# Two products of a gated linear attention in 64x64 matmul tiles instead of 64x128

## The chip, the cores and the metric

The kernel runs on one core of a Trainium2 chip. TensorE (PE) multiplies matrices into PSUM; a matmul instruction is preceded by a load of its stationary operand (LDWEIGHTS, shown as PEld). VectorE (DVE), ScalarE (ACT) and GpSimd (POOL) do the elementwise work, and SyncE (SP) issues most of the DMAs. The metric is the device time of one launch in microseconds (us); a comparison of the two kernels resolves about 2%.

## The reference

Per batch and head a 48x48 state is decayed row by row and updated with an outer product at each of 768 steps; the output of a step is the query times the state. The result, 3072 tokens by 384, goes through a gated feed-forward layer.

```python
B, H, S, D = 4, 8, 768, 48
f = 1 / (1 + exp(-f_logit))
for t in range(S):
    state = f[:, :, t, :, None] * state + einsum('bhd,bhe->bhde', k[:, :, t], v[:, :, t])
    y[:, :, t] = einsum('bhd,bhde->bhe', q[:, :, t], state)
x = y.transpose(0, 2, 1, 3).reshape(B * S, H * D)        # 3072 x 384
h = x @ w_in                                             # 384 -> 2048
out = (h * sigmoid(h)) @ w_out                           # 2048 -> 384
```

## The kernel before, in words

The 768 steps are cut into 3 windows of 256 steps, and each window into two chunks of 128. With 4 batches that makes 12 blocks, D = 0 to 11 (window D // 4, batch D % 4). In a block a partition holds a pair of neighbouring steps, r = 0 and 1; partitions 0 to 63 are the first chunk and 64 to 127 the second (f = 0 and 1 in the matmuls). The decays become factors on q and k, so that inside a chunk the attention is a masked product of q and k times v, and only the state is carried from chunk to chunk.

The order of all work is written out by hand in a long string, PLAN, whose tokens are emitted one after the other; a token such as `Y.8.0` is a step kind, a block and a half of the heads (g = 0 or 1, four heads each). Each engine takes its instructions in that order. Buffers come from small pools by class, also decided by the order of the tokens. The steps that matter here:

- SC (line 350): scores q times k, in tiles of 48 rows by 64 columns of the array, 128 moving columns; the two heads of a pair stand on two row halves, the two chunks on two column halves. 16 matmuls per token, 24 tokens.
- AT (line 356, DVE): the mask times the scores, out of PSUM.
- Y (line 364): the second attention product, masked scores times v. The contraction is over the 64 partitions of a chunk f, so two matmuls use the upper and the lower half of the array; each writes 128 partitions (both r of the 64 output pairs) by the 48 columns of one head. 16 matmuls per token, 24 tokens.
- YS (line 371): q times the carried state, added onto Y's PSUM banks, in tiles of 128 rows by 64 columns, 96 moving columns. 8 matmuls per token, 20 tokens.
- YC (line 278): copies the sum out of PSUM.
- DP (line 389): the state product, k times v over a chunk. Two heads x of a pair n are stationary together (128 columns of the array) and both heads' values move (96 columns), so the result is a 128x96 block for each pair whose two off-diagonal quarters belong to no head. 16 matmuls per token for blocks 0 to 7; in the last window only the first chunk is needed, and blocks 8 to 11 have 8 (the function `chunks_with_state`).
- SD (line 394, DVE): adds DP's PSUM bank to the carried state. SU (line 396, POOL or DVE): multiplies by the decay `al`, which is zero in the off-diagonal quarters, and writes the new state in bf16.
- MI and MO (lines 405 and 418): the two feed-forward products, full 128x128 tiles with 256 and 384 moving columns; SI (line 413, ACT) the gate between them.
- W (line 443): products of zeros, in the first part of the kernel alone.

`nc.tensor.matmul` issues one LDWEIGHTS and one MATMUL each time. Where the operands start on partition 64, or where the output does, decides which part of the array is used.

## Time and profile before

| | us |
|---|---|
| median of 3 runs | 176.93 (176.51 to 178.69) |
| profiled execution, whole | 176.33 |
| its span from first to last instruction | 174.61 |
| PE busy | 168.4 |
| ACT / DVE / POOL busy | 123.4 / 101.7 / 72.1 |

The span is what the profile's views divide up; the profiled execution took 1.7 us more than its span. PE's busy time overlaps itself, because a matmul starts streaming while the one ahead is still draining; how fast matmuls follow each other is therefore read from the chain of work that ended last, whose rows give a group of instructions the time until the next group begins. The names in the rows: `ps` is a PSUM bank, `atm` the masked scores, `vb` the values v, `qk` the factored q and k before transposition, `qkT` after it, `st` the state, `sd` state plus product, `yb` the copied output, `hT` the hidden layer.

### The profile page before, as it was taken

Reading aid. Unit: us, or ns where it says so; the run is one execution under the profiler, and the core shown is the slowest. Engines: PE = TensorE matmul, PEld = TensorE weight load, DVE = VectorE, ACT = ScalarE, POOL = GpSimd, SP = SyncE. Lnnn points to the kernel's source line nnn. Section 1 sums busy time; section 2 is a strip of 40 time slices with the busy share of each in tenths; the row PEclk is TensorE's granted clock in tenths of the full one; section 3 lists DMA queues with packets and bytes.
Section 4 is the critical chain, followed back from the end, with each engine's and each line's share of the span. In section 5 each row is a group of like instructions: output and inputs, shape, how many; then the busy total and the mean of one; then the engine's idle time right before and its main releaser. Section 6 shows DMA issues by size and latency. Waiting matters only on the chain.

```text
span 174.6 us, 5617 instructions
## 1 busy us (share of the span) xinstructions
PE 168.4 (96%) x2289; PEld 128.6 (74%) x2289; DVE 101.7 (58%) x248; ACT 123.4 (71%) x287; POOL 72.1 (41%) x121
## 2 busy tenths in 40 slices
PE   7799999999999999999999999999999999999992
PEld 5677788867856788867688767688667788867671
DVE  6389989666447989488494597893678400000010
ACT  5989999898948989696987948769621227763420
POOL 6486752519891784213229260193019220000220
PEclk9999999999999999999999999999999999999999
DMA  5999999999949959999798999899994683000064
GB/s 136 278 283 303 329 350 357 351 277 357 299 93 222 302 137 266 127 272 300 131 282 156 267 271 263 185 223 238 302 108 88 159 168 90 4 0 0 0 144 132
DMA packets 81066, 36.02 MB, mean 206 GB/s; under 512 B 74000, under 2 KB 80272, under 8 KB 81040
## 3 DMA queue, kind: packets, MB, share of 16 engines
q1 hardware_dynamic: 79440, 31.86, 74.6%
q0 software_dynamic: 1024, 3.15, 6.9%
q10 hardware_dynamic: 576, 0.66, 1.1%
q8 instruction: 18, 0.29, 0.7%
q14 instruction: 8, 0.07, 0.1%
HBM read 25.17 MB, written 4.72 MB: 171 GB/s over the span
## 4 chain that ended last, share of the span: by engine, by line
PE 83%; SPq 9%; DMA 4%; DVE 1%; issue 1%; ACT 0%; ACTq 0%
PE ps L418 36%; PE ps L405 33%; SPq L282 7%; DMA wide<-in_k_dram 4%; PE ps L350 3%; PE ps L364 3%; PE ps L371 2%; SPq L434 2%; PE ps L389 2%; PE ps L337 1%; PE ps L298 1%; DVE qk L328 1%; PE ps L379 0%; PE ps L302 0%; DVE wide L317 0%
## 5 line engine op out<-in xcount | busy, mean ns | idle before, releaser
L418 PE MATMUL ps<-w_out_sb,hT 128*128 128x384 bf16 (+2 forms) x400 | 68.1, 320 | 0.0
L405 PE MATMUL ps<-xT,w_in_sb 128*128 128x256 bf16 x576 | 67.1, 273 | 0.0
L405 PEld LDWEIGHTS <-w_in_sb 128*128 128x128 bf16 x576 | 55.4, 98 | 8.6 <-POOL w_in_sb L278 0.2
L413 ACT ACTIVATE hT<-ps 128x512 bf16<-128x512 f32 x88 | 45.8, 626 | 14.7 <-PE ps L405 14.3
L418 PEld LDWEIGHTS <-hT 128*128 128x128 bf16 x400 | 36.9, 98 | 20.7
L356 DVE TENSOR_TENSOR atm<-ps,mask 128x512 bf16<-128x512 f32 x48 | 29.9, 683 | 13.0 <-PE ps L350 12.8
L278 DVE COPY o<-ps 128x384 f32<-128x384 f32 (+1 forms) x11 | 5.9, 541 | 32.2 <-PE ps L418 32.2
L426 POOL DMA_DIRECT2D out_dram<-o x16 | 9.9, 619 | 29.7 <-ACT o L278 26.3
L278 ACT COPY o<-ps 128x384 f32<-128x384 f32 (+1 forms) x14 | 6.4, 465 | 16.2 <-PE ps L418 16.2
L396 POOL TENSOR_TENSOR st<-sd,al 128x384 bf16<-128x384 f32 x13 | 10.9, 845 | 11.9 <-DVE sd L394 11.9
L284 ACT ACTIVATE e<-wide 128x384 f32<-128x384 f32 x24 | 12.2, 520 | 4.7 <-DMA wide<-in_f_logit_dram 3.8
L328 POOL TENSOR_TENSOR qk<-wide,ia 128x192 bf16<-128x192 f32 x22 | 13.2, 621 | 5.4 <-DVE wide L317 4.7
L328 DVE TENSOR_TENSOR qk<-wide,ps 128x192 bf16<-128x192 f32 x48 | 14.1, 347 | 1.7 <-ACT ps L311 0.8
L290 POOL TENSOR_TENSOR s<-lf 128x192 bf16<-128x192 bf16 x15 | 8.5, 578 | 14.3 <-ACT lf L286 14.2
L317 POOL TENSOR_TENSOR wide<-wide,f 128x192 f32<-128x192 f32 x14 | 9.0, 639 | 13.2 <-DMA wide<-in_k_dram 12.2
L328 DVE TENSOR_TENSOR qk<-wide,ia 128x192 bf16<-128x192 f32 x26 | 12.5, 527 | 1.8 <-POOL wide L317 1.7
L319 DVE SCALAR_TENSOR_TENSOR wide<-e,wide 128x192 f32<-128x192 f32 x24 | 10.1, 434 | 4.8 <-DMA wide<-in_q_dram 4.8
L286 ACT ACTIVATE lf<-e 128x384 bf16<-128x384 f32 x24 | 12.2, 525 | 0.3
L447 ACT ACT_TABLE_LOAD x9 | 11.5, 1283 | 0.2
L443 PE MATMUL ps<-idle 128*128 128x256 bf16 x65 | 10.3, 318 | 1.3 <-DVE idle L455 1.3
L278 POOL CAST vb<-wide 128x768 bf16<-128x768 f32 x7 | 6.0, 873 | 12.5 <-DMA wide<-in_v_dram 12.5
L394 DVE TENSOR_TENSOR sd<-ps,st 128x384 f32<-128x384 f32 x16 | 8.3, 551 | 4.0 <-ACT hT L413 2.7
(60 smaller groups left out, 176.1 us busy)
## 6 DMA issues: line engine op xcount, KB each, us to landing
wide<-in_f_logit_dram SPq DMA_DIRECT2D x10, 384.0 KB, 5.0
wide<-in_q_dram SPq DMA_DIRECT2D x10, 384.0 KB, 6.1
wide<-in_k_dram SPq DMA_DIRECT2D x10, 384.0 KB, 5.5
wide<-in_v_dram SPq DMA_DIRECT2D x10, 384.0 KB, 5.5
wide<-in_moe_w_in_dram SPq DMA_DIRECT2D x8, 384.0 KB, 6.1
wide<-in_moe_w_out_dram SPq DMA_DIRECT2D x8, 384.0 KB, 5.9
out_dram<-o POOLq DMA_DIRECT2D x16, 192.0 KB, 3.9
wide<-in_f_logit_dram SPq DMA_DIRECT2D x4, 192.0 KB, 3.3
```

The source lines that it names most:

```text
L278: copy = lambda o, i: E.copy(o, i) if eng == "a" else E.tensor_copy(o, i)
L282: E.dma_start(out=T[0][:, hs], in_=SRC[kind[2]][w, b][:, hs])
L284: nc.scalar.activation(T[1][:, hs], T[0][:, hs], AF.Exp, scale=-1.0)
L286: nc.scalar.activation(T[1][:, hs], T[0][:, hs], AF.Ln, bias=1.0)
L328: E.tensor_mul(T[2][:, g, int(kind == "KI"), :, r, :, 0:d], T[0][:, hs, r * d:r * d + d].rearrange("p (n x) d -> p n x d", x=2), decay.rea ...
L356: nc.vector.tensor_mul(T[2][:, g, x], T[x].rearrange("p (s n c) -> p s n c", s=2, n=2), mask.rearrange("p s r c -> p s (r c)")[:, :, None, ...
L396: E.tensor_mul(T[2].rearrange("p n (x d) -> p n x d", d=d), T[0][:, 0:HD].rearrange("p (n x d) -> p n x d", n=4, d=d) if "ps" in mine[0] e ...
L405: nc.tensor.matmul(h[:, i, 128 * fs.start:128 * fs.stop], w_in_sb[:, j, kk, i * 128:i * 128 + 128], T[0][:, fs, kk], start=(kk == 0), stop ...
L413: nc.scalar.activation(T[1][:, 2 * j:2 * j + 2], T[0].rearrange("p (n c) -> p n c", n=2), AF.Silu)
L418: nc.tensor.matmul(T[1][:, 0:cols.stop - cols.start], T[0][:, n, f * 128:f * 128 + 128], w_out_sb[:, n, cols], start=(n == 0), stop=(n == ...
L443: nc.tensor.matmul(T[0][:, 0:256], idle[:, 0:128], idle[:, 0:256], start=True, stop=True, skip_group_check=True)
L447: nc.scalar.preload_act_table_set(turn[name])
```

## The change

Y and DP are issued in 64x64 tiles. In Y each matmul becomes two, one for each half r of its 128 output partitions; the moving operand (48 columns of v) is the same for both. In DP each matmul becomes two, one for each head x of the pair, and each moves only that head's 48 columns, so the off-diagonal quarters are no longer computed: a state bank holds, on 64 partitions per head, 4 x 48 columns instead of 4 x 96. SD (and SU for the first chunk) read those columns with a stride of zero, so that the 128x384 tile they write has a copy in both places of a pair; the one that belongs to the wrong head is multiplied by the zero in `al`, as before.

```diff
+        heads = lambda x: x.rearrange("p n (x d) -> p n x d", d=d)
+        both_heads = lambda x: x[:, 0:4 * d].rearrange("p (n d) -> p n d", d=d)[:, :, None, :].to_broadcast([128, 4, 2, d])
...
                         for f in range(2):
-                            nc.tensor.matmul(T[2 + f][:, h * d:h * d + d], T[0][64 * f:64 * f + 64, g, x, s, n],
-                                             T[1][64 * f:64 * f + 64, h, s * d:s * d + d],
-                                             start=(h == 0 and s == 0), stop=True, skip_group_check=True)
+                            for r in range(2):
+                                nc.tensor.matmul(T[2 + f][64 * r:64 * r + 64, h * d:h * d + d],
+                                                 T[0][64 * f:64 * f + 64, g, x, s, n, 64 * r:64 * r + 64],
+                                                 T[1][64 * f:64 * f + 64, h, s * d:s * d + d],
+                                                 start=(h == 0 and s == 0), stop=True, skip_group_check=True)
...
                     for f in fs:
-                        nc.tensor.matmul(T[2 + f][:, 2 * d * n:2 * d * n + 2 * d],
-                                         T[0][64 * f:64 * f + 64, n // 2, 1, n % 2, r].rearrange("p x c -> p (x c)"),
-                                         T[1][64 * f:64 * f + 64, 2 * n:2 * n + 2, r * d:r * d + d],
-                                         start=(n == 0 and r == 0), stop=True, skip_group_check=True)
+                        for x in range(2):
+                            nc.tensor.matmul(T[2 + f][64 * x:64 * x + 64, d * n:d * n + d],
+                                             T[0][64 * f:64 * f + 64, n // 2, 1, n % 2, r, x],
+                                             T[1][64 * f:64 * f + 64, 2 * n + x, r * d:r * d + d],
+                                             start=(n == 0 and r == 0), stop=True, skip_group_check=True)
         elif kind == "SD":
-            nc.vector.tensor_add(T[1], T[0][:, 0:HD].rearrange("p (n c) -> p n c", n=4), T[2])
+            nc.vector.tensor_add(heads(T[1]), both_heads(T[0]), heads(T[2]))
         elif kind == "SU":
-            E.tensor_mul(T[2].rearrange("p n (x d) -> p n x d", d=d),
-                         T[0][:, 0:HD].rearrange("p (n x d) -> p n x d", n=4, d=d) if "ps" in mine[0] else T[0].rearrange("p n (x d) -> p n x d", d=d),
+            E.tensor_mul(heads(T[2]), both_heads(T[0]) if "ps" in mine[0] else heads(T[0]),
                          T[1][:, :, a[1]][:, :, :, None].to_broadcast([128, 4, 2, d]))
```

On PE the place where the state products of block 6 end and the scores of block 6 begin (`DP.6 SC.6.0` in PLAN) stands before the change as follows; the two numbers behind a name are partitions by columns of the output, and `ps_130` and `ps_133` are the banks of the two chunks.

```order
L389 LDWEIGHTS qk_99
L389 MATMUL ps_133<-vb_104,qk_99 128x96
L389 LDWEIGHTS qk_99
L389 MATMUL ps_130<-vb_104,qk_99 128x96
L389 LDWEIGHTS qk_99
L389 MATMUL ps_133<-vb_104,qk_99 128x96
L350 LDWEIGHTS qkT_107 [waits DMAHW0_49]
L350 MATMUL ps_131<-qkT_107 64x128 [waits Activation_49]
```

And the same place in the changed kernel, where the lines are numbered 2 to 5 higher:

```order
L394 LDWEIGHTS qk_99
L394 MATMUL ps_130<-vb_104,qk_99 64x48
L394 LDWEIGHTS qk_99
L394 MATMUL ps_130<-vb_104,qk_99 64x48
L394 LDWEIGHTS qk_99
L394 MATMUL ps_133<-vb_104,qk_99 64x48
L394 LDWEIGHTS qk_99
L394 MATMUL ps_133<-vb_104,qk_99 64x48
L352 LDWEIGHTS qkT_107 [waits DMAHW0_49]
L352 MATMUL ps_131<-qkT_107 64x128 [waits Activation_49]
```

Each pair of instructions has become two pairs on the same bank with half the output partitions and half the columns; the waits, the banks and what follows are the same.

On PE the place where the second attention products of block 8 begin behind a feed-forward product (`MO.6.0.2 ... Y.8.0` in PLAN), before the change; `ps_133` and `ps_127` are the banks of the two chunks:

```order
L418 LDWEIGHTS hT_118
L418 MATMUL ps_132<-w_out_sb,hT_118 128x384
L364 LDWEIGHTS atm_108
L364 MATMUL ps_133<-vb_102,atm_108 128x48 [waits DVE_49]
L364 LDWEIGHTS atm_108
L364 MATMUL ps_127<-vb_102,atm_108 128x48 [waits DVE_49]
```

And in the changed kernel, at the same place:

```order
L422 LDWEIGHTS hT_118
L422 MATMUL ps_132<-w_out_sb,hT_118 128x384
L367 LDWEIGHTS atm_108
L367 MATMUL ps_133<-vb_102,atm_108 64x48 [waits DVE_49]
L367 LDWEIGHTS atm_108
L367 MATMUL ps_133<-vb_102,atm_108 64x48
L367 LDWEIGHTS atm_108
L367 MATMUL ps_127<-vb_102,atm_108 64x48 [waits DVE_49]
L367 LDWEIGHTS atm_108
L367 MATMUL ps_127<-vb_102,atm_108 64x48
```

The two matmuls of a round, one for each chunk, have become four, two for each chunk, with the same columns and the waits at the same bank's first matmul.

Over the whole program PE has 5668 rows instead of 4580: 384 more matmuls from Y, 160 more from DP, each with its load. The rows of DVE, ACT, POOL and SP are the same in both kernels, in order, shapes and waits, and PE's waits stand at the same matmuls.

## The prediction

> **What bounds the kernel now.** I read the page's head first, then the shares of the chain of work that ended last, then that chain in order of time.

> ```profile
> span 174.6 us, 5617 instructions
> PE 168.4 (96%) x2289; PEld 128.6 (74%) x2289; DVE 101.7 (58%) x248; ACT 123.4 (71%) x287; POOL 72.1 (41%) x121
> PE 83%; SPq 9%; DMA 4%; DVE 1%; issue 1%; ACT 0%; ACTq 0%
> PE ps L418 36%; PE ps L405 33%; SPq L282 7%; DMA wide<-in_k_dram 4%; PE ps L350 3%; PE ps L364 3%; PE ps L371 2%; SPq L434 2%; PE ps L389 2%; PE ps L337 1%; PE ps L298 1%; DVE qk L328 1%; PE ps L379 0%; PE ps L302 0%; DVE wide L317 0%
> PEclk9999999999999999999999999999999999999999
> ```

> PE is 96% busy, 83% of the chain is PE, and the clock row shows full speed in every slice. What is not PE lies at the start:

> ```profile
> 17.91 6.97 DMA wide<-in_k_dram
> 26.61 0.88 PE ps L337 x11
> 171.19 0.03 ACTq L278
> ```

> Until 26.6 us the chain is loads. From 26.61 to 171.19 us it is PE alone, so whatever PE gains or loses there moves the end by as much, and what it gains earlier does not. The two lines that are changed carry 3% and 2% of the chain (L364 is Y, L389 is DP). How many of their matmuls lie behind 26.61 us the table by stage says, for L364 and then for L389:

> ```profile
> 26.61:174.61 148.00, 5.78 (x320) 4.88 (x320) 1.00 0.81 193
> 26.61:174.61 148.00, 4.41 (x128) 3.57 (x128) 1.00 0.81 193
> ```

> So 320 of Y's 384 and 128 of DP's 160 matmuls count.

> **How long a round takes now.** I call a round the matmuls that stand on different parts of the array at the same time. The chain's rows give rounds by differences, since the first of a stretch also pays for a change of tile size:

> ```profile
> 55.30 0.79 PE ps L389 x32
> 56.09 0.40 PE ps L364 x32
> 71.90 0.79 PE ps L389 x32
> 72.69 0.35 PE ps L350 x16
> 75.75 0.79 PE ps L350 x48
> 79.90 0.91 PE ps L364 x64
> 80.81 0.80 PE ps L371 x32
> 97.28 0.57 PE ps L350 x32
> 130.78 0.68 PE ps L389 x16
> 137.13 0.63 PE ps L371 x24
> ```

> - Y, two row halves, 48 columns: at 56.09 us Y follows DP in the same tile size, and 16 pairs take 0.40 us, 25.0 ns a pair. At 79.90 us 32 pairs take 0.91, which is 0.80 and 0.11 for the change of size ahead.
> - DP, 96 columns: at 130.78 us only one chunk is computed, and 16 matmuls, one at a time, take 0.68 us, 42.5 ns each. At 55.30 us 32 matmuls are 16 pairs: 0.79 less 0.11 is 0.68 again. The second matmul of a pair is free.
> - YS, two column halves, 96 columns: 8 matmuls more cost 0.80 - 0.63 = 0.17, 42.5 ns a pair. Column halves run side by side as well.
> - SC, four tiles (two rows by two columns), 128 columns: 16 matmuls more cost 0.79 - 0.57 = 0.22, 55 ns for a round of four. This is the one four-tile row here.

> From 96 to 128 columns a round grows by 13 ns, 0.41 ns a column; 96 columns are then 39 and the surplus 3 ns, while Y's 48 columns are 20 and the surplus 5.

> **The change part by part.** A round of Y now takes two matmuls and will take four; a round of DP takes two (one in the last window) and will take four (two). The number of rounds stays: on the chain 160 of Y, and of DP 48 pairs in blocks 2 to 7 and 32 single ones in blocks 8 to 11, together 80. They cost 160 x 25.0 + 80 x 42.5 = 4.0 + 3.4 = 7.4 us. Afterwards all 240 move 48 columns in 64x64 tiles and last some time P, so the term is **0.240 P - 7.4 us**, zero at P = 30.8 ns. DP wins by halving its columns, Y can only lose.

> P is in no row: four tiles are seen with 128 columns only (55 ns), 48 columns with two tiles only (25 ns). These are its ends; below 25 it can't be expected, since each tile streams the same 48 columns as a tile of Y does now. In between the weights decide:

> ```profile
> L364 PEld LDWEIGHTS <-atm 64*128 64x128 bf16 x384 | 5.9, 93 | 1.4 <-issue 1.2
> L350 PEld LDWEIGHTS <-qkT 48*64 48x64 bf16 x384 | 5.8, 106 | 2.4 <-issue 1.6 <-ACT qkT L278 0.2
> L389 PEld LDWEIGHTS <-qk 64*128 64x128 bf16 x160 | 4.4, 94 | 1.5 <-issue 1.1 <-ACT o L278 0.3
> L371 PEld LDWEIGHTS <-qkT 128*64 128x64 bf16 x160 | 4.0, 109 | 0.5 <-issue 0.2
> ```

> A load of 64 columns takes 106 to 109 ns and one of 128 columns 93 to 94: half the columns, yet 13 to 15 ns more. If a 64-column load advances a column per step as the moving data do, it needs 64 x 0.41 = 26 ns in the array, an estimate from the rows above, and the 128-column load about half of that. Within a round of 55 or 42.5 ns this is hidden behind the streaming; within one of 20 ns of streaming it is not. With the surplus of 3 ns that rounds show, P is 29 to 30. I take **P = 30**, nearer to Y's 25 because 48 columns are Y's case: 0.240 x 30 = 7.2, **-0.2 us**, of which Y is +0.8 and DP -1.0.

> [...]

> Smaller terms. At 72.69 us SC follows DP; the first four rounds take 0.35 where four more cost 0.22, so a change of size costs about 0.1 us. DP and SC will have the same 64x64 size; on the chain this happens twice (`DP.6 SC.6.0`, `DP.7 SC.7.0`): -0.2. Stretches of Y and DP begin behind another tile size 9 times on the chain, the first and the last of them here:

> ```profile
> 32.09 0.30 PE ps L364 x16
> 136.62 0.51 PE ps L364 x32
> ```

> The first load of a stretch is not hidden: 9 x 14 ns = +0.1. The last matmuls of a round of four start later than those of a pair: under 0.1. Together about 0.

> SD and SU: the DVE and POOL rows keep their count and output shapes.

> ```profile
> L394 DVE TENSOR_TENSOR sd<-ps,st 128x384 f32<-128x384 f32 x16 | 8.3, 551 | 4.0 <-ACT hT L413 2.7 <-PE ps L389 0.6 <-ACT o L278 0.5
> L396 DVE TENSOR_TENSOR st<-ps,al 128x384 bf16<-128x384 f32 x4 | 2.2, 553 | 0.9 <-PE ps L389 0.6 <-ACT o L278 0.3
> ```

> SU from PSUM already reads its decay with a stride of zero and takes 553 ns against SD's 551, so I cost the new reading at nothing. Its cover is DVE's idle 42% of the span; the least it could do is read half the columns faster, and were an SD as slow as half again (0.28 us x 16), the state would still come before YS asks as far as the chain tells, which from 26.6 us on has no step of DVE or POOL in it. No wait is added anywhere; what queues behind Y (YS, then YC on DVE or ACT) shifts by the rounds' 0.1 us per stretch.

> Sum: -0.2 us, from the profiled execution's 176.33 to 176.1. That execution lies 0.6 under the median, 176.93, and both kernels are judged by medians, so the forecast is **176.7 us**; its own range, P from 27 to 34, is -0.9 to +0.8, 176.0 to 177.7.

> **The rivals.**

> *A round of 25 ns.* If the load hides after all, Y costs what it does and DP falls to 25: 0.240 x 25 - 7.4 = -1.4, 175.5 us. For it: every load seen so far is hidden. Against it: none so far had only 20 ns to hide behind.

> *The load comes on top.* Perhaps Y's 25 ns is already its load, 13 ns and some 12 for the swap. Then 13.5 ns more give P = 38.5: +1.8, 178.8 us. For it: Y's surplus of 5 ns is larger than the 3 of the others. Against it: a surplus of 2 ns is little to build on.

> *Four at once is not four.* This ends on the slower side. If the two column halves of one row half take turns when rounds are short, or if a four-tile round has a floor that does not depend on the columns, P is 2 x 25 = 50 up to SC's 55: +4.6 to +5.8, 181.5 to 182.7 us. It decides for slower by 2% (3.5 us) from P = 45 on. For it: SC at 55 is the only four-tile row there is. Against it: 128 columns alone explain the 55 by 0.41 ns a column, and YS shows column halves side by side. [...]

> *PE runs out of instructions.* A row of the page's queues, and one of the chain:

> ```profile
> q8 instruction: 18, 0.29, 0.7%
> 62.69 9.21 PE ps L405 x84
> ```

> 18 packets for PE's 4578 instructions are 254 each, and 0.7% of 16 engines' 174.6 us are 1.1 us a packet. At 30 ns a round of eight instructions, 254 are used up in 0.95 us, less than a packet takes; now Y uses them in 1.6 us. Four tokens of Y with YS behind them (79.9, 104.8 and 130 to 133 us) might each wait up to a us: +1 to +2.5 on top, about 178.4 us. Against it: between such stretches a matmul of MI takes 9.21 / 84 = 0.11 us, so 254 instructions last 14 us, and the supply stands ahead when a stretch begins.

> **How the numbers follow.** The forecast 0.50; round of 25 ns 0.15; load on top 0.15; instructions run out 0.07; four is not four 0.11; 0.02 for something unseen. The range leaves out the four-is-not-four case and little more: from the 25 ns case less the 0.4 to 0.6 us by which runs fall below the median, 174.9, to the load-on-top case with about a us for runs above it, 180.0. Two percent, about what a measurement of this kernel tells from no change, is 3.5 us: faster by that would need P under 17, below the 20 ns of streaming, 0.02; slower needs the last rival or two of the others together, 0.13; within, 0.85.

> **What would show it.** In the chain after, the four tokens of Y near 80 us as 128 matmuls in 0.96 + 0.11 = 1.07 us where 64 took 0.91, the two DP tokens near 72 us as 64 in about 0.6 where 32 took 0.79, and SC.6.0 behind them nearer 0.22 than 0.35; the loads of L367 and L394 at 106 to 109 ns. Y at 1.7 us would be the turn-taking, at 0.91 the hidden load, and rounds at 30 with gaps between them the instruction supply. I am wrong if P is not near 30, or if DVE's SD rows leave 551 ns and PE begins to wait for `st`.

## The result, and the profile after

The changed kernel takes **191.69 us** (median of 6 runs, 189.58 to 193.02) against 177.55 us (6 runs) for the kernel before: 1.077 times as long, 95% interval 1.067 to 1.086. The forecast was 176.7 us, at most 180.0. The ratio is taken over the runs of each kernel within 1.5% of its fastest. The profiled execution took 192.75 us with a span of 191.0, so its sums are about a us larger than the median's.

The head of the page after, its clock row, the shares of the chain, one of its groups and the row of the queue that brings instructions (L367 is Y in the changed kernel; L394, in the chain below, is DP):

```profile
span 191.0 us, 6705 instructions
PE 175.8 (92%) x2833; PEld 133.4 (70%) x2833; DVE 101.0 (53%) x248; ACT 124.2 (65%) x287; POOL 72.0 (38%) x121
PEclk9999759999999979999999999999996699999999
PE 83%; issue 5%; SPq 4%; DMA 3%; ACT 2%; DVE 1%; ACTq 0%; DVEq 0%
L367 PE MATMUL ps<-vb,atm 64*64 64x48 bf16 x768 | 9.4, 189 | 6.2 <-issue 6.2
q8 instruction: 22, 0.36, 0.8%
```

PE is busy for 92% instead of 96%. Two things are new: 5% of the chain is "issue", time in which PE waits for nothing that the profile shows, and the granted clock, full in every slice before, sags in three places. The chain in order of time shows both (start, length, what):

```profile
18.92 0.63 PE ps L367 x42
19.55 3.82 issue
23.37 0.52 PE ps L367 x13
...
35.86 2.79 PE ps L409 x24
...
63.44 0.34 PE ps L352 x13
63.78 2.19 issue
65.97 0.53 PE ps L352 x19
66.51 1.39 PE ps L422 x4
...
82.62 0.65 PE ps L394 x64
83.27 0.23 PE ps L352 x15
...
86.22 0.80 PE ps L352 x48
...
115.41 1.16 PE ps L367 x128
...
142.16 0.76 PE ps L367 x85
142.92 2.35 issue
145.26 0.25 PE ps L367 x3
...
147.62 5.32 PE ps L422 x20
152.94 0.63 PE ps L367 x64
```

PE stops three times in the middle of a token, for 3.82, 2.19 and 2.35 us: the first and third inside a Y, the second inside an SC, whose code is not changed at all. Behind each stop the matmuls themselves are slow: 4 of MO (L422) take 1.39 us at 66.51 where the same 4 took 0.76 before, 20 take 5.32 where 20 took 3.36. The table by stage has the clock of these stretches (length, PE busy, PEclk, DMA share, GB/s):

```profile
21.90:28.70 6.80, 5.33 (x61) 0.50 1.10 345
66.30:69.70 3.40, 3.40 (x26) 0.51 0.91 234
144.80:151.60 6.80, 6.33 (x73) 0.50 0.65 126
```

Three rows of the chain of before, for the same 24 matmuls of MI, the same 4 and the same 20 of MO:

```profile
29.36 2.73 PE ps L405 x24
...
57.42 0.76 PE ps L418 x4
...
133.26 3.36 PE ps L418 x20
```

Against the chain of before, the same 24 matmuls of MI start at 35.86 instead of 29.36 us (+6.5), the same 48 of SC at 86.22 instead of 75.75 (+10.5), the same two tokens of Y at 152.94 instead of 136.62 (+16.3), and the chain of PE ends at 187.66 instead of 171.19 (+16.5). The loss lies in three steps of 6.5, 4.0 and 5.8 us, one at each stop, and almost nothing lies elsewhere. The second step is 2.19 of stop and 3.4 / 2 = 1.7 of half clock; the third 2.35 and 3.4. The first is 3.82 and part of 3.4, since up to 26.6 us loads had been the chain before.

The rounds, by contrast, are nearly what was forecast. Four tokens of Y take 1.16 us at 115.41, that is (1.16 - 0.11) / 32 = 33 ns a round; two of DP with SC behind them take 0.65 + 0.23 where 0.79 + 0.35 stood.

### The profile page after: what moved, and what is told of

The parts are those of the page before. It is cut to its first block, busy times and chain, and to the rows that moved or that the text cites. A ratio compares the mean times of both kernels' runs of the same rounds, so it can differ in the third digit from the quotient of the medians.

```text
span 191.0 us, 6705 instructions
## 1 busy us (share of the span) xinstructions
PE 175.8 (92%) x2833; PEld 133.4 (70%) x2833; DVE 101.0 (53%) x248; ACT 124.2 (65%) x287; POOL 72.0 (38%) x121
## 4 chain that ended last, share of the span: by engine, by line
PE 83%; issue 5%; SPq 4%; DMA 3%; ACT 2%; DVE 1%; ACTq 0%; DVEq 0%
PE ps L422 35%; PE ps L409 33%; PE ps L367 4%; SPq L284 4%; PE ps L352 3%; PE ps L375 3%; DMA wide<-in_f_logit_dram 3%; PE ps L394 2%; PE ps L383 1%; PE ps L300 1%; PE ps L339 1%; DVE qkT L280 1%; DVE w_in_sb L280 1%; ACT e L286 1%; ACT qkT L280 1%
## 5 line engine op out<-in xcount | busy, mean ns | idle before, releaser
L422 PE MATMUL ps<-w_out_sb,hT 128*128 128x384 bf16 (+2 forms) x400 | 71.3, 330 | 0.0
L409 PE MATMUL ps<-xT,w_in_sb 128*128 128x256 bf16 x576 | 68.3, 276 | 0.2 <-DVE w_in_sb L280 0.2
L409 PEld LDWEIGHTS <-w_in_sb 128*128 128x128 bf16 x576 | 56.3, 99 | 9.0 <-DVE w_in_sb L280 0.4
L417 ACT ACTIVATE hT<-ps 128x512 bf16<-128x512 f32 x88 | 46.3, 626 | 18.1 <-PE ps L409 17.7
L422 PEld LDWEIGHTS <-hT 128*128 128x128 bf16 x400 | 37.9, 100 | 22.5 <-issue 3.0
L367 PE MATMUL ps<-vb,atm 64*64 64x48 bf16 x768 | 9.4, 189 | 6.2 <-issue 6.2
L280 DVE CAST yb<-ps 128x384 bf16<-128x384 f32 x12 | 6.4, 555 | 14.2 <-PE ps L375 7.1
L367 PEld LDWEIGHTS <-atm 64*64 64x64 bf16 x768 | 8.0, 107 | 7.8 <-issue 7.5
L330 DVE TENSOR_TENSOR qk<-wide,ia 128x192 bf16<-128x192 f32 x26 | 11.0, 471 | 2.2 <-POOL wide L319 2.2
```

Of the source, the lines that this page charges most:

```text
L280: copy = lambda o, i: E.copy(o, i) if eng == "a" else E.tensor_copy(o, i)
L330: E.tensor_mul(T[2][:, g, int(kind == "KI"), :, r, :, 0:d], T[0][:, hs, r * d:r * d + d].rearrange("p (n x) d -> p n x d", x=2), decay.rea ...
L367: nc.tensor.matmul(T[2 + f][64 * r:64 * r + 64, h * d:h * d + d], T[0][64 * f:64 * f + 64, g, x, s, n, 64 * r:64 * r + 64], T[1][64 * f:64 ...
L409: nc.tensor.matmul(h[:, i, 128 * fs.start:128 * fs.stop], w_in_sb[:, j, kk, i * 128:i * 128 + 128], T[0][:, fs, kk], start=(kk == 0), stop ...
L417: nc.scalar.activation(T[1][:, 2 * j:2 * j + 2], T[0].rearrange("p (n c) -> p n c", n=2), AF.Silu)
L422: nc.tensor.matmul(T[1][:, 0:cols.stop - cols.start], T[0][:, n, f * 128:f * 128 + 128], w_out_sb[:, n, cols], start=(n == 0), stop=(n == ...
```

## The experiments

Two theories were put against each other from the first experiment on. By S, the supply, PE can run only as far as its instructions have arrived, which come in packets of about 256 (22 on q8 in the page after, for 5666 loads and matmuls), and stops where it gets through them faster than the next packet comes. By T, the tiles, the stops belong to the four-tile rounds. What suggested S is a count. The table by stage gives, up to the beginning of each stop, the stretch, its length, and the busy time and count of PE's matmuls, then of its loads, then of DVE, ACT and POOL:

```profile
0.00:19.50 19.50, 16.22 (x351) 12.69 (x352) 14.06 (x47) 15.94 (x38) 11.98 (x29) 1.00 0.92 244
0.00:63.70 63.70, 56.41 (x990) 43.73 (x991) 40.46 (x104) 49.17 (x111) 34.48 (x63) 0.95 0.88 251
0.00:142.90 142.90, 133.41 (x2397) 102.22 (x2397) 95.36 (x238) 107.01 (x254) 64.42 (x109) 0.96 0.91 229
```

Loads and matmuls together are 703, 1981 and 4794. The differences are 1278 and 2813, 5 and 11 times 256 less 2 and 3: all three stops stand, to within 5, on one ladder, 447 + 256 k (703, 1983, 4799). I call its steps rungs.

**One product at a time.** Each half of the change alone, with the other as before.

```diff
 DP alone (L392): 64x64 tiles as in the change; Y (L366) in 64x128 as before
 Y alone (L366):  64x64 tiles as in the change; DP (L391) in 64x128 as before
```

> Theory S (supply): PE's instructions arrive in packets of 256, and PE can run only to its 447th load or matmul plus 256 for each packet that has landed; where 320 instructions run in less than about 5 us, the next packet is late and PE stops for the rest. Theory T (tiles): the stops and the slow clock come from the four-tile rounds themselves, wherever there are many. Here DP alone is in 64x64 tiles, Y is as before: 4900 rows on PE. S: the shortest 320 instructions take 4.2 us (near 57 us), the others 5.8 and more, so at most one stop of about 1 us; the rounds of DP at 33 ns instead of 42.5 save 80 x 9.5 ns = 0.8 us; 176 to 177.5 us against 177.5 before. T: stops in proportion, some of the 14 us, 180 us and more.

> Y alone in 64x64 tiles, DP as before: 5348 rows on PE. S: 320 instructions take 2.5 us near 134 us, 3.2 near 20 us and 4.8 near 81 us, so stops of 2 to 3 us at the first two, after 703 and after 447 + 16 x 256 = 4543 loads and matmuls, each with a few us of half clock behind it; rounds of 33 ns instead of 25 cost 160 x 8 ns = 1.3 us: 185 to 189 us. T: nearly the whole loss, 189 to 192 us, and stops anywhere.

DP alone is level with the kernel before: ratio 1.001, 0.997 to 1.006. Its profile has one stop on the ladder, after 702 loads and matmuls, with 1.27 us on the chain, which is more than the 0.8 us that the rounds save. Y alone takes 1.046 times as long (1.037 to 1.055), 185.16 us. Its stops, counted in the table by stage of that kernel:

```profile
0.00:20.00 20.00, 17.25 (x351) 13.40 (x352) 15.81 (x50) 17.07 (x42) 13.93 (x32) 1.00 0.97 267
0.00:141.80 141.80, 135.12 (x2269) 102.62 (x2269) 96.51 (x239) 107.41 (x256) 65.24 (x112) 0.98 0.94 231
```

They stand after 703 and 4538, the rungs that S had named (703 and 4543), and are 3.21 and 1.35 us long on the chain. Y alone and DP alone lose 7.6 and 0 us by their medians, both together 14: the loss is not a sum over tiles.

**The same number of instructions without the tiles.** The kernel before, with an idle matmul behind each one of Y and DP.

```diff
                             nc.tensor.matmul(T[2 + f][:, h * d:h * d + d], T[0][64 * f:64 * f + 64, g, x, s, n], ...)
+                            nc.tensor.matmul(T[2 + f][:, HD + 1:HD + 2], T[0][64 * f:64 * f + 64, g, x, s, n],
+                                             T[1][64 * f:64 * f + 64, h, 0:1], start=False, stop=True, skip_group_check=True)
 (the same behind each matmul of DP)
```

> The kernel before in its 64x128 tiles, but each matmul of Y and DP is followed by one more with the same weights and a single moving column, written to a column of the bank that nobody reads: 5668 rows on PE, as in the changed kernel, and no 64x64 tile beyond SC's. The added rounds cost about 25 ns each, 240 x 25 = 6 us. S: stops after the same 703, 1983 and 4799 loads and matmuls as in the changed kernel, somewhat shorter since a stretch takes longer (320 instructions in 3.1, 4.3 and 2.9 us), with half clock behind them: 188 to 195 us. T: no stop at all: 183 us.

194.50 us, 1.094 times the kernel before (1.081 to 1.106). The table by stage of this kernel, up to its three stops:

```profile
0.00:20.00 20.00, 17.04 (x351) 13.35 (x352) 14.09 (x48) 16.59 (x40) 13.32 (x32) 1.00 0.95 259
0.00:64.50 64.50, 58.39 (x990) 45.73 (x991) 38.91 (x104) 49.19 (x111) 34.68 (x63) 0.95 0.88 251
0.00:146.80 146.80, 139.14 (x2397) 108.07 (x2397) 93.30 (x238) 107.13 (x254) 65.11 (x111) 0.97 0.88 222
```

Exactly the matmuls of the changed kernel, 351, 990 and 2397, without any new 64x64 tile. T had no stop here. Its stops are 3.54, 1.55 and 1.05 us long. So it was the number of instructions that brought the stops here, not the tiles.

**The same kernel, 112 instructions later.** Only the first products of zeros differ, whose results nothing uses.

```diff
         elif kind == "W":
-            for _ in range(D):
-                nc.tensor.matmul(T[0][:, 0:256], idle[:, 0:128], idle[:, 0:256], ...)
+            count, width = (76, 64) if D == 20 else (D, 256)
+            for _ in range(count):
+                nc.tensor.matmul(T[0][:, 0:width], idle[:, 0:128], idle[:, 0:width], ...)
```

> The changed kernel, but the first 20 products of zeros (256 columns each) are 76 of 64 columns, the same columns in all: PE gets 112 more instructions at the very start, where it only warms up, and every later instruction stands 112 places further back. Tiles, order and the rest are untouched. S: the places where a packet is late move by 112 instructions: one stop stays near 18 us (320 instructions in 2.9 us), those at 64 and 143 us go or shrink under 1 us (4.4 to 5.2 us), and with them their half clock: 180 to 185 us. T: the same 191 us as the changed kernel, with stops at the same tokens.

189.92 us (ratio 1.062, 1.049 to 1.074), and its three longest stops are after 703, 2237 and 4027 loads and matmuls, 3.70, 0.38 and 3.18 us on its chain: rungs again (2239 and 4031), so the stops stay at the counts and change their place in the work. As forecast the one near 64 us shrank and the one at 143 us went. But a new one came at 113.6 us, where none had been forecast, and the time lies 5 us above the range forecast: S told the rungs, not which of them would be late by how much.

**All of the change that lies on the chain, at two phases.** Y and DP in 64x64 tiles from block 2 on, 320 and 128 matmuls behind 26.6 us before the change. The two kernels differ in the products of zeros at the start alone, 44 of 116 columns or 100 of 52.

```diff
+                        if D < 2:    # (Y and DP: as before)
...
+                        else:        # (Y and DP: as in the change)
...
+            count, width = (44, 116) if D == 20 else (D, 256)      # the one kernel
+            count, width = (100, 52) if D == 20 else (D, 256)      # the other
```

> Y and DP in 64x64 tiles from block 2 on, which is all of the change that lies on the chain; blocks 0 and 1 as before. The first 20 products of zeros (256 columns) are 44 of 116, nearly the same columns, 48 instructions more, so that the packets' limits fall outside the dense stretches: 5524 rows on PE. Theory S (supply): 320 instructions ahead of a limit take at least 4.4 us, so stops of at most a us or so in all and little or no half clock; rounds of 32 to 33 ns give 0.240 x 32.5 - 7.4 = +0.4 us: 177.5 to 180 us. Theory T (the four-tile rounds cause the loss): most of the 14 us, 187 us and more.

> The kernel of e9_late_good with 100 products of 52 columns at the start instead of 44 of 116: the same tiles, order and columns, 112 more instructions ahead of everything. S: now 320 instructions take 1.9 us ahead of the 1983rd (near 57 us) and of the 4799th (near 133 us), so PE stops there after 1983 and 4799 loads and matmuls for 2 to 4 us each, with half clock behind them: 5 to 12 us slower than e9_late_good. T, or no dependence on the place in the stream: the same time as e9_late_good.

181.81 us (ratio 1.026, 1.020 to 1.031; 180.89 to 184.62) and 194.92 us (191.38 to 195.72): 112 instructions at the start, before any of the work, cost 13 us by the medians and 10.5 by the fastest run of each. The first kernel lies above the 177.5 to 180 us that S had named, but far below the 187 of T. The stops of the second kernel on its chain:

```profile
35.98 1.93 issue
62.58 3.00 issue
92.44 2.29 issue
148.58 1.44 issue
```

They stand after 1213, 1981, 3004 and 4794 loads and matmuls; two of these rungs were named. A fifth, 0.81 us after 703, is not on the chain. The first kernel has one long stop, 2.33 us, after 3771 (rung 3775), and 3.4 us at half clock behind it:

```profile
110.21 2.33 issue
...
112.30:115.70 3.40, 3.16 (x34) 0.50 0.11 26
```

The 2.33 and half of 3.4 are 4.0 us. The median is 4.4 above the kernel before, but the sum can't be set against it to the tenth: this execution took 184.62 us and also waits 1.26 us, near 104 us, for a DMA that transposes q and k; others of the six had full clock, 181.7 and 183.2 us.

**Fewer and better placed.** Y in 64x64 tiles in 7 of the 10 late blocks, DP in all ten, at a phase that was worked out to leave at least 5.2 us for 320 instructions.

```diff
-                            if D < 2:
+                            if D not in (2, 3, 4, 5, 6, 7, 10):
...
-            count, width = (44, 116) if D == 20 else (D, 256)
+            count, width = (52, 98) if D == 20 else (D, 256)
```

> As e9_late_good, but Y in 64x64 tiles in blocks 2 to 7 and 10 alone (224 of the 320 matmuls on the chain), DP from block 2 on, and the first 20 products of zeros as 52 of 98 columns: 5348 rows on PE, as many as Y alone had. The blocks and the start are chosen so that 320 instructions ahead of a packet's limit take 5.2 us or more everywhere. Theory S (supply): no stop of more than 0.5 us, full clock; rounds of Y cost 112 x 7.5 ns = 0.8 us, of DP save 80 x 10 ns = 0.8 us: the time of the kernel before within 1 us, 176.5 to 179 us. Theory T: at least half of the 14 us, 184 us and more.

181.30 us, ratio 1.020 (1.013 to 1.027), the expectation missed. The profiled execution has full clock in every slice, but a stop of 2.14 us after 3771 once more, near 108 us, and one of 0.85 after 702. Placing by a fixed time for 320 instructions isn't enough: the 320 ahead of rung 3775 took 8.3 us here with the stop in them, those at the three stops of the changed kernel 6.3, 5.8 and 4.1.

**DP alone, late, at two phases.** DP in 64x64 tiles from block 2 on, Y as before; then the same with 92 products of 56 columns at the start.

```diff
+                        if D < 2:    # (DP: as before)
...
+                        else:        # (DP: as in the change)
...
+            count, width = (92, 56) if D == 20 else (D, 256)       # the second kernel alone
```

> DP in 64x64 tiles from block 2 on, blocks 0 and 1 and all of Y as before: 4836 rows on PE. Theory S (supply): 320 instructions never take less than 5.3 us, so no stop, in particular none after the 703rd, where DP alone lost 1.3 us; 80 rounds of DP at 33 ns instead of 42.5 save 0.76 us, less about 0.3 for new changes of size between DP and Y: 0.4 to 0.8 us faster than before, ratio 0.995 to 0.998. Theory T (tiles cause the loss): slower than before, as DP alone or worse.

> The kernel of e5_dp_late, but the first 20 products of zeros (256 columns) are 92 of 56, nearly the same columns: 144 more instructions at the very start, every later one 144 places further back. S: now 320 instructions in front of the 4287th take 2.7 us, near 132 us, so PE stops there for 1 to 2.5 us, possibly with a few us of half clock behind it: 178 to 182 us, 1 to 4 us slower than e5_dp_late. T, or no dependence on the place of instructions in the stream: the same time as e5_dp_late.

The first is level with the kernel before, ratio 1.001 (0.997 to 1.005), at full clock, its longest stop on a rung 0.38 us on the chain. The gain of 0.4 to 0.8 us that was expected is not to be seen, though the rounds are as short as they should be: two tokens of DP take 0.65 us (0.79 before). Its profile has two waits of PE for a DMA that transposes (qkT), 0.89 us near 77 and 0.56 near 103 us, which the profile of the kernel before does not have; whether they took the gain in the other runs too is not shown. The second, with 144 instructions more at the start, takes 182.01 us, 1.024 times the kernel before (1.017 to 1.032) and 4.2 us above the first: the sign expected and about the size, but not the place. Its stop at the rung of 4287 was only 0.4 us; the longest was one after 703, near 19 us, 1.95 us on the chain, with 3.4 us of half clock behind it. Part of the 4.2 us need not be the supply's: this profile has three waits for transposing DMAs, 0.83, 0.76 and 0.58 us.

**The rounds by themselves.** The kernel before with six series of 12 rounds on zeros at its end, one run.

```diff
+        for _ in range(12):
+            for f in range(2):
+                for r in range(2):
+                    nc.tensor.matmul(banks[f][64 * r:64 * r + 64, 0:48], idle[64 * f:64 * f + 64, 64 * r:64 * r + 64],
+                                     idle[64 * f:64 * f + 64, 0:48], start=True, stop=True, skip_group_check=True)
 (and with 2 and 80 columns; two column halves, 48; two row halves, 2; two 64x64 tiles of one column half, 48)
```

> The kernel before, with six series of 12 rounds at its end, on zeros, each behind 24 products of 512 columns: four 64x64 tiles with 2, 48 and 80 columns; two column halves (128x64) with 48; two row halves (64x128) with 2; two 64x64 tiles on one column half with 48. If the load of 64 columns sets the round: four tiles 33 ns at 2 and at 48 columns, 36 to 37 at 80; column halves with 48 also 33; row halves 25. If the rate of issue does (8 instructions in 33 ns): four tiles 33 at 2 columns, but two tiles with 64-column loads well under 33. If streaming does: four tiles at 2 columns well under 33.

The chain of this kernel, in the order of the series (four tiles with 2, 48 and 80 columns; column halves with 48; row halves with 2; two tiles with 48):

```profile
179.82 0.48 PE ps L490 x48
...
185.58 0.49 PE ps L496 x48
...
191.36 0.55 PE ps L502 x48
...
197.20 0.49 PE ps L507 x24
...
202.98 0.39 PE ps L512 x24
...
208.65 0.49 PE ps L517 x24
```

Each holds 12 rounds and a change of size of 0.1 us. A round of four tiles takes (0.48 - 0.10) / 12 = 32 ns with 2 columns, 32 with 48 and 37 with 80; two tiles with 64-column loads 32 as well, so up to 48 columns neither the columns nor the number of tiles decides. The row halves, with their 128-column loads, take 24. What the rounds of 32 ns have in common is the load of 64 columns, and that it sets them is the reading that fits all six series; no series has a 64-column load on the whole width of the array, so the load isn't told apart from the column half that goes with it.

**A pause of PE that has its instructions.** The kernel before, with PE made to wait for four multiplications on DVE ahead of `MO.4.1.0`.

```diff
+            if name == "MO.4.1.0":
+                nc.tensor.matmul(T[1][:, 0:2], idle[:, 0:128], idle[:, 0:2], ...)
+                nc.vector.tensor_copy(pause[:, 0:2], T[1][:, 0:2])
+                for _ in range(4):
+                    nc.vector.tensor_mul(pause, pause, pause)
+                nc.tensor.matmul(T[1][:, 0:2], pause[:, 0:128], pause[:, 0:2], ...)
```

> The kernel before, with one made pause of PE: ahead of MO.4.1.0 (near 73 us) a product of zeros waits for four multiplications on DVE, about 2.5 us in which PE has its instructions and does nothing; 4 more rows on PE. If the clock falls because PE idles, whatever for: the pause and a stretch of 3.4 or 6.8 us at half clock, 2.5 + 1.7 to 3.4, 181 to 183.5 us. If the half clock belongs to the late instructions or the tiles: 2.5 alone, 180 us, full clock throughout.

The row of PE's timeline that ends the pause (start, length, what, and the idle time before it):

```profile
75.18 0.18 PE L422 MATMUL ps<-pause 128*128 128x2 bf16 x1 [2.09 <-DVE pause L421]
```

180.25 us, ratio 1.015 (1.009 to 1.022). The profiled execution has the full clock throughout and loses the pause and, near 103 us, 0.65 us at a wait for a transposing DMA. Of the four runs two had a mean clock of 0.987 and 0.990, about 4 us of half clock in 178, and two 0.999 and more. That does not yet show that the pause lowers the clock: of the 18 runs of the kernel before that were taken beside these, without a pause, two had 0.990 and 0.991.

Whether a given stop brings half clock is not settled by its length: in the changed kernel 2.19 us brought 3.4 us of it, in the kernel with idle matmuls a stop of 1.05 us did too (mean clock 0.97 up to it, 0.964 over the span), and in Y alone one of 1.35 us brought none (0.98 up to it, 0.982 over the span). What the trace of the changed kernel does show is a grid: its granted clock changes only at whole steps of 3.41 us (half clock begins at 21.88, 66.25 and 144.76 us, 13 and 23 steps apart, and ends 2, 1 and 2 steps later). The table by stage for three stretches of that length (length, PE busy, PEclk, DMA share, GB/s): the one at the stop after 3771 in the kernel with 44 products at its start, and the two at the same stop in the kernel with fewer tiles (52 products):

```profile
108.85:112.27 3.42, 1.36 (x135) 1.00 0.68 200
105.06:108.47 3.41, 2.87 (x132) 1.00 1.03 309
108.47:111.88 3.41, 1.81 (x14) 1.00 1.04 168
```

The stop of 2.33 us leaves PE idle for 2.06 us of the first, and half clock follows; the stop of 2.14 us is split over the other two into 0.54 and 1.60, and none does. In the changed kernel the steps ahead of half clock have 2.33, 2.19 and 1.84 us of idle PE; the step from 4.81 us on has 1.29 us, and full clock follows. From 1.05 us (the stop in the kernel with idle matmuls) to 1.60 us both were seen. A second step at half clock came where PE was idle for 1.49 and 0.51 us of the first, which makes the 6.8 us, and none where it was idle for 0.00 (66.25 us) or 0.24 us (the kernel with 44 products). It came without a stop of the supply too: in the kernel before the last matmul ends at 171.2 us, and the clock is 1.00 up to 176.1 and 0.50 from 176.2 us on.

## Why the prediction was wrong

**The bound** was read rightly: PE alone from 26.6 us on, with nothing to cover for it.

**The round** was forecast at P = 30 ns from the load of 64 columns; the series by itself gives 32 and the changed kernel 33. The term becomes 0.240 x 33 - 7.4 = +0.5 us instead of -0.2. The reading fits the series, 32 ns with 64-column loads and 24 with 128-column loads, though the load is not told apart there from the column half, and the rivals of 25, 38 and 50 to 55 ns fall: four tiles take the 32 ns that two take.

**The size changes** that go: SC behind DP takes 0.23 us instead of 0.35. Right. **SD and SU** keep their durations. Right; the rows of the page after:

```profile
L399 DVE TENSOR_TENSOR sd<-ps,st 128x384 f32<-128x384 f32 x16 | 8.3, 550 | 5.1 <-ACT hT L417 4.1 <-PE ps L394 0.9
L401 DVE TENSOR_TENSOR st<-ps,al 128x384 bf16<-128x384 f32 x4 | 2.2, 553 | 0.9 <-PE ps L394 0.7 <-ACT o L280 0.2
```

**The step that failed** is the rival "PE runs out of instructions": named, with the row of queue q8 that carries it, and then put at 1 to 2.5 us with a chance of 0.07. Two of its sentences were wrong. "The supply stands ahead when a stretch begins" took a long slow stretch for a reserve. The ladder speaks against any reserve beyond a fixed number of packets: the stops stand at 447 + 256 k, to within 5, whatever was done before (703, 1981 and 4794 in the changed kernel). And a packet was priced at its own 1.1 us. Of the three places that it named, only one had a stop, the Y at 130 to 133 us before (142.92 after); the Y at 90.37 and 115.41 us after ran without, and the stops near 20 and 64 us were not named. The trace has the packet of the second stop between 63.7 and 64.6 us (the queues of the changed kernel in that window):

```profile
q1 hardware_dynamic: 712, 0.27, 111.3%
q8 instruction: 1, 0.02, 6.1%
```

PE had stopped at 63.78 and goes on at 65.97, 1.4 us after the packet is in. This holds all along the traces before and after: PE passes rung 447 + 256 k only when packet number k + 1 of q8 has been in for at least 1.29 us, and the three stops of the changed kernel end 1.3, 1.4 and 1.5 us behind their packets (in at 22.08, 64.59 and 143.78 us). Before the stop, 161 matmuls with their loads, 322 instructions, run in 3.45 us; in the densest stretch ahead of a rung in the kernel before (1727), 167 run in 5.85 us and nothing stops:

```profile
60.15:63.60 3.45, 3.45 (x161) 1.00 0.97 241
55.33:61.18 5.85, 5.85 (x167) 1.00 1.13 304
```

So what has to be compared with the 3.45 us of the stretch is the time until PE may go on, 3.45 + 2.2 = 5.6 us, not 1.1. The kernel before passes by a narrow margin: its packet for that rung was in 1.9 us ahead of PE, at 59.3 us, where the three stops ended 1.3 to 1.5 us behind theirs. The change doubled the instructions just where they are densest.

**What was not named at all** is the clock. I had read it as full and kept it full. Each of the three stops is followed by 3.4 or 6.8 us at half clock, 17 us together, which costs up to 8.5 us, as much as the stops' 8.4.

**Open.** What a packet waits for is not shown: the loads' queue q1 alone has packets for 111% of the 16 engines' time in that window (their times overlap), and no run here takes the input loads away from the packets. The third stop came without full DMA engines, though: they were busy for 22% of the time (141.35 to 144.76 us), and PE stopped all the same, behind 320 instructions in 1.6 us. Nor could I forecast which rung is late: stops of 2 to 3 us came where none or less than a us had been expected. The waits for transposing DMAs told above took 0.6 to 1.3 us each; such DMAs (of qkT or xT) stand on the chains of nine of the experiments and on neither that of the kernel before nor that of the changed one, and what brings the waits was not followed up.

## What to carry to other kernels

Where small matmuls stand densely, count instructions per us as well as columns: here the 320 loads and matmuls ahead of a late packet's rung took 3.5 to 8.3 us, the stop included, and the change, which halves the tile and doubles the count, paid for it in whole stops, not in the rounds. A stop of PE must be priced with the half clock that may follow, 1.7 or 3.4 us more here, and a stop in code that no one has changed, at a fixed count of instructions, was the mark of the supply here. If the sum of a change on PE comes to a few tenths of a us, the risk is in what its instructions do to the rest.
